# Splitting decoded weights and the gate's sigmoids placed behind the PSUM evictions, and weights decoded 512 columns at a time

## The chip, the cores and the metric

The kernel runs on one core of one Trainium2 chip. The metric is the device time of one execution in microseconds (us). PE is the tensor engine, DVE the vector engine, ACT the scalar engine, POOL is GpSimd, and SP issues the DMAs. Each engine works through its own list of instructions in order. An instruction that waits holds up everything behind it on its engine.

## The reference

Three blocks follow each other for a batch of 4, with 8 heads, 576 positions, head size 64 and 512 channels.

```python
# attention: one full softmax over 4-fold averaged q, k, v, repeated 4 times,
# plus one softmax over the band |i - j| < 4
attn_out = out_up + out_local                      # x: (4, 576, 512)
# gate
gate = sigmoid(causal depthwise conv of x, 5 taps)
x = (gate * (x @ w_val)) @ w_out
# mixing over positions, then over channels
h = relu(x.T @ w_tok1) @ w_tok2                    # 576 -> 256 -> 576
u = x + h.T
out = u + relu(u @ w_ch1) @ w_ch2                  # 512 -> 1536 -> 512
```

The weights of the last two blocks are float64 in memory; all else is float32.

## The kernel before, in words

**Products in three passes.** Each large operand is kept as two tiles: `hi`, the value rounded to the format that PE multiplies fast, and `lo`, the rest. `mm3` adds hi·hi, hi·lo and lo·hi (lines 194, 195 and 196), so each product of a tile is three matmuls.

**Decoding weights.** `decode` fetches a chunk of float64 words into a tile `w64` (named `w` in the trace), lets DVE put together the float32 bits in a tile `wa` by three instructions (L124, L125, L127), lets ACT copy these into `hi` with rounding (L130), and lets POOL subtract to get `lo` (L131). The buffers `w64` and `wa` exist `NWD` times each. A chunk is `WB` columns wide. `w_ch1` is decoded block by block during batch 0 (`ch1_new`, 12 blocks `f`, tile `w_hl`) and written to DRAM (`w_dr`); later batches read it back. Blocks are asked for `AHEAD` = 4 ahead of use. `w_ch2` (tile `ch`) is decoded late in the program.

**Stages.** Attention of batch 0 runs by itself (0 to about 83 us), with idle matmuls on PE between its pieces (`busy`). Then a program of PE's instructions, fixed by hand, runs over the batches: `p1(b)` (value product `p_val`, gate, output product `p_x`, transposes, `r_ps`, `p_h`) and `c1(b)` (the products `g_ps` with `w_ch1`), with the attention of batch `b+1` mixed in at fixed places. The last product with `w_ch2` (`p_o`) fills the time from about 512 us on. PE's order is written out by `mix` and `first_products`. The order on the other engines is made by a scheduler from the order of the code and priorities (`tc.high_priority`).

**Evictions.** ACT takes finished sums out of PSUM: `u_sb` (L494), `x_hl` of the transposes (L504), `r_hl` (L543), `r_sb` (L585), and the attention's `pts_d`, `pts_l` (L295, L343). PE cannot reuse a bank before its eviction. ACT also takes the exponentials of the softmax (`e_d`, `e_l`, L234) and the sigmoids of the gate (L375). Exponential and sigmoid live in different function tables; each change between them is one `ACT_TABLE_LOAD`.

**DVE** besides the decoding does the maxima `mx` of the softmax (L228), the sums `x_f` (L360), the convolution `gate_sb` (L365, L370), the gated product `y` (L481), `lo` parts, and `u_sb` + `p_h` (L558).

Of the kernel before, what the change touches and what calls it, by code (L numbers as in the profile page):

```python
# [34 lines left out]
TAPS = 5  # L35
WB = 256
NW = 16
# [14 lines left out]
FETCH = 10  # L52
NW0, NW1 = 8, 3
NXY = 2
# [5 lines left out]
NPT = 3  # L60
NY = 3
NV = 2
NV4 = 1
ND = 2
NVD = 2
NWD = 3
NX2 = 4
# [7 lines left out]
def kernel(ctx, tc, qk, vw, v4, w_val, conv_w, w_out, w_tok1, w_tok2, w_ch1, w_ch2, out):  # L75
# [25 lines left out]

    idle = T(sb, [128, 512], BF16, "idle", 1, name="idle")
    nc.vector.memset(idle, 0.0)

    def busy(n):
        for _ in range(n):
            p = T(ps, [128, 512], F32, "ao", BANKS["ao"], name="idle_ps")
            nc.tensor.matmul(p, lhsT=idle[:, 0:128], rhs=idle, start=True, stop=True)

# [4 lines left out]

    def decode(src, n, rows, hi, lo, full=None, shape=None):
        x = T(sb, [128, n, 2], I32, "w64", NWD, name="w64")[0:rows]
        a = T(sb, [128, n], I32, "wa", NWD, name="wa")[0:rows]
        if shape is None:
            nc.sync.dma_start(out=x, in_=src.bitcast(I32).rearrange("p (n t) -> p n t", t=2))
        else:  # L120
            nc.sync.dma_start(out=x.rearrange("p (k n) t -> p k n t", k=shape[0]),
                              in_=src.bitcast(I32).rearrange("p k (n t) -> p k n t", t=2))
        low, high = x[:, :, 0], x[:, :, 1]
        nc.vector.tensor_scalar(a, high, 3, 0x3FFFFFF8, ALU.logical_shift_left, ALU.bitwise_and)  # L124
        nc.vector.scalar_tensor_tensor(out=a, in0=high, scalar=-0x40000000, in1=a,  # L125
                                       op0=ALU.bitwise_and, op1=ALU.bitwise_or)
        nc.vector.scalar_tensor_tensor(out=a if full is None else full.bitcast(I32), in0=low, scalar=29, in1=a,  # L127
                                       op0=ALU.logical_shift_right, op1=ALU.bitwise_or)
        if full is None:
            nc.scalar.activation(out=hi, in_=a.bitcast(F32), func=AF.Copy)  # L130
            nc.gpsimd.tensor_tensor(out=lo, in0=a.bitcast(F32), in1=hi.bitcast(F32), op=ALU.subtract)  # L131

    def load_w(key, pieces, tag, bufs, parts=None):

        for j, group in enumerate(pieces):
            n = group[0][1].shape[1]
            hi, lo = parts or [T(sb, [128, len(group), n], F32R, tag, bufs, name=f"{key}{j}_{p}") for p in ("hi", "lo")]
            for i, (rows, src) in enumerate(group):
                for c in range(0, n, WB):
                    e = min(n, c + WB)  # L140
# [33 lines left out]
    def ch2_new():  # L174
# [3 lines left out]
        for tag, bufs in slots:  # L178
            if tag == "w2":
                pairs = [[T(sb, [128, 1, DM], F32R, tag, bufs, name=f"ch2_{f}_{p}")[:, 0] for p in range(2)]]  # L180
            else:
                n = 1 if tag == "wt1" else 2
                t = T(sb, [128, n, 2, DM], F32R, tag, bufs, name=f"ch2_{f}")
                pairs = [[t[:, i, p] for p in range(2)] for i in range(n)]
            for hl in pairs:
                wt["ch2", f] = hl
                for c in range(0, DM, 256):
                    decode(w_ch2[f * 128:f * 128 + 128, c:c + 256], 256, 128, *[t[:, c:c + 256] for t in hl])
                    yield
# [51 lines left out]
    def attention(b):  # L241
# [89 lines left out]
        def loc_turn(hp):  # L331
# [3 lines left out]
            for c0, c1 in LU:  # L335
# [6 lines left out]
                with early():  # L342
                    nc.scalar.activation(out=t, in_=p, func=AF.Copy)  # L343
                ts += [t[:, j] for j in range(n)]

        def loc_out(hp):
# [3 lines left out]
            for j, t in enumerate(ts):  # L350
                for par in range(2):
                    r0 = 64 * par
                    for h in range(2):
                        nc.tensor.matmul(ps_o[par][64 * h:64 * h + 64, j, :],
                                         lhsT=v[r0:r0 + 64, j, 64 * h:64 * h + 64],
# [16 lines left out]

        def sigmoid(s0=0, s1=S):
            for g in g_t:
                nc.scalar.activation(out=g[:, s0:s1], in_=g[:, s0:s1], func=AF.Sigmoid)  # L375

        if b:
# [5 lines left out]
            for i in range(NHP + 1):  # L383
# [20 lines left out]
                if i + 1 < NHP:  # L404
                    hpd[i + 1]["v"] = load_v(b, i + 1)
            sigmoid()
            return

        L = 2
        for hp in range(NHP + L):  # L410
# [11 lines left out]
            if hp >= L:  # L422
# [6 lines left out]
                if hp == NHP + L - 1:  # L429
                    conv(hp - L, 0, HS)  # L430
                    sigmoid(0, HS)
                    conv(hp - L, HS, S)
                else:
                    conv(hp - L)
                yield
        sigmoid(HS, S)
        yield
# [25 lines left out]
    def p1(b):  # L463
# [12 lines left out]
        def val(hs, c, x, y2):  # L476
            p = bank(P1T["p_val"], "p_val")
            cxs(p, wv, x, c)
            with first():
# [4 lines left out]
        def outs(hs, y2):  # L484
            for c0 in (0, 2):
# [83 lines left out]
    def c1(b):  # L569
# [6 lines left out]
        for f in range(NFT):  # L576
            w1 = ws.pop(f)
            r = T(sb, [128, S], F32, "r", 2, name="r_sb")
            for hs in range(2):
# [143 lines left out]
```

## Time and profile before

| | |
|---|---|
| median of 3 runs | 666.13 us (665.65 to 666.78) |
| profiled execution | 664.67 us |
| its span, first to last instruction | 662.8 us |
| PE busy | 622.3 us, 94% |
| DVE, ACT, POOL busy | 339.4, 316.4, 210.0 us |
| mean granted TensorE clock | 0.972 |

The span is what the trace shows; 1.9 us of the execution lie outside it. The profiled execution is 1.5 us under the median of the runs. Busy times of different engines overlap. A clock of 1.00 is 2.4 GHz and 0.50 is 1.2 GHz, so a mean below 1 says for how much of the time PE ran at the lower level.

### The profile page before, as it was taken

Reading aid. Unit: us, or ns where it says so; the run is one execution under the profiler, and the core shown is the slowest. Engines: PE = TensorE matmul, PEld = TensorE weight load, DVE = VectorE, ACT = ScalarE, POOL = GpSimd, SP = SyncE. Lnnn points to the kernel's source line nnn. Section 1 sums busy time; section 2 is a strip of 40 time slices with the busy share of each in tenths; the row PEclk is TensorE's granted clock in tenths of the full one; section 3 lists DMA queues with packets and bytes.
Section 4 is the critical chain, followed back from the end, with each engine's and each line's share of the span. In section 5 each row is a group of like instructions: output and inputs, shape, how many; then the busy total and the mean of one; then the engine's idle time right before and its main releaser. Section 6 shows DMA issues by size and latency. Waiting matters only on the chain.

```text
span 662.8 us, 12825 instructions
## 1 busy us (share of the span) xinstructions
PE 622.3 (94%) x4911; PEld 529.6 (80%) x4911; DVE 339.4 (51%) x630; ACT 316.4 (48%) x1044; POOL 210.0 (32%) x242
## 2 busy tenths in 40 slices
PE   8999778897979999999999999999998999999997
PEld 3444477785878988998998999998897888888887
DVE  3679999775686465442344434117635242324232
ACT  1758457485548586546656843324433222222221
POOL 5564655336536422614231323205513000000000
PEclk8999798797979999999999999999999999999999
DMA  7744226623675244784322586565898345454221
GB/s 254 235 143 117 76 81 205 217 75 122 221 244 178 87 150 131 242 245 124 105 72 72 146 255 203 160 195 187 252 355 272 96 144 174 142 176 127 80 74 38
DMA packets 53900, 107.23 MB, mean 162 GB/s; under 512 B 5776, under 2 KB 21392, under 8 KB 53840
## 3 DMA queue, kind: packets, MB, share of 16 engines
q1 hardware_dynamic: 53840, 106.42, 51.1%
q8 instruction: 38, 0.62, 0.4%
q14 instruction: 22, 0.18, 0.1%
HBM read 76.52 MB, written 29.88 MB: 161 GB/s over the span
## 4 chain that ended last, share of the span: by engine, by line
PE 60%; DVE 6%; DMA 5%; ACT 3%; issue 2%; POOL 1%; SPq 0%; DVEq 0%; ACTq 0%
PE p_o L194 7%; PE p_o L196 7%; PE p_o L195 7%; PE g_ps L194 5%; PE g_ps L195 5%; PE g_ps L196 5%; DMA w<-in_w_ch_dram 4%; PE sc_l L325 2%; PE p_x L194 2%; DVE wa L124 2%; PE p_x L195 2%; PE p_x L196 2%; PE p_val L194 2%; PE p_val L196 2%; PE p_val L195 2%
## 5 line engine op out<-in xcount | busy, mean ns | idle before, releaser
L194 PE MATMUL g_ps<-u_hl,w_hl 128*128 128x288 f32 x384 | 117.8, 307 | 0.0
L195 PE MATMUL g_ps<-u_hl,w_hl 128*128 128x288 f32 x384 | 115.0, 299 | 2.1 <-POOL u_hl L444 1.9
L196 PE MATMUL g_ps<-u_hl,w_hl 128*128 128x288 f32 x384 | 113.9, 297 | 0.0
L194 PE MATMUL p_o<-g_hl,ch 128*128 128x512 f32 (+1 forms) x240 | 88.8, 370 | 2.2 <-ACT r_sb L585 2.1
L196 PE MATMUL p_o<-g_hl,ch 128*128 128x512 f32 (+1 forms) x240 | 88.5, 369 | 0.0
L195 PE MATMUL p_o<-g_hl,ch 128*128 128x512 f32 (+1 forms) x240 | 88.5, 369 | 0.0
L443 ACT ACTIVATE g_hl<-r_back 128x512 fp32r<-128x512 f32 (+1 forms) x60 | 35.3, 589 | 109.1 <-PE p_o L196 106.3
L444 DVE TENSOR_TENSOR g_hl<-r_back,g_hl 128x512 fp32r<-128x512 f32 (+1 forms) x60 | 39.4, 658 | 92.8 <-ACT g_hl L443 89.6
L195 PEld LDWEIGHTS g_ps<-u_hl,w_hl 128*128 128x128 f32 x384 | 73.3, 191 | 3.5 <-POOL u_hl L444 3.5
L194 PEld LDWEIGHTS g_ps<-u_hl,w_hl 128*128 128x128 f32 x384 | 73.1, 190 | 3.1 <-issue 1.7
L196 PEld LDWEIGHTS g_ps<-u_hl,w_hl 128*128 128x128 f32 x384 | 73.2, 191 | 0.0
L370 DVE SCALAR_TENSOR_TENSOR gate_sb<-x_f,cw,gate_sb 128x575 f32<-128x575 f32 (+5 forms) x68 | 62.8, 930 | 1.5 <-ACT gate_sb L367 0.5
L585 ACT ACTIVATE r_sb<-g_ps 128x288 f32<-128x288 f32 x96 | 38.2, 406 | 47.0 <-PE g_ps L196 41.2
L124 DVE TENSOR_SCALAR wa<-w 128x256 int32<-128x256 int32 (+2 forms) x76 | 37.1, 499 | 34.8 <-DMA w<-in_w_ch_dram 21.1
L194 PEld LDWEIGHTS p_o<-g_hl,ch 128*128 128x128 f32 x240 | 45.2, 188 | 10.8 <-ACT r_sb L585 3.2
L196 PEld LDWEIGHTS p_o<-g_hl,ch 128*128 128x128 f32 x240 | 45.2, 188 | 7.7
L195 PEld LDWEIGHTS p_o<-g_hl,ch 128*128 128x128 f32 x240 | 45.3, 189 | 7.6
L234 ACT ACTIVATE e_l<-sc_l,mx 128x64 f32<-128x64 f32 x160 | 48.1, 331 | 0.4
L194 PE MATMUL p_x<-y_hl,out_hi 128*128 128x288 f32 x128 | 40.9, 320 | 4.2 <-ACT u_sb L494 3.7
L125 DVE SCALAR_TENSOR_TENSOR wa<-w,wa 128x256 int32<-128x256 int32 (+2 forms) x76 | 44.2, 591 | 1.1
L444 POOL TENSOR_TENSOR x_hl<-x_f,x_hl 128x288 fp32r<-128x288 f32 x32 | 27.7, 877 | 45.5 <-ACT x_hl L443 44.8
L194 PE MATMUL p_val<-x_hl,val_hi 128*128 128x288 f32 x128 | 39.5, 309 | 1.4 <-DVE y L481 0.7
(108 smaller groups left out, 1354.0 us busy)
## 6 DMA issues: line engine op xcount, KB each, us to landing
w_hl<-w_dr SPq DMA_DIRECT2D x36, 512.0 KB, 4.6
r_dr<-r_sb SPq DMA_DIRECT2D x48, 288.0 KB, 4.6
w<-in_w_ch_dram SPq DMA_DIRECT2D x48, 256.0 KB, 3.4
r_back<-r_dr SPq DMA_DIRECT2D x48, 256.0 KB, 3.0
qk_sb<-in_qk_dram SPq DMA_DIRECT2D x16, 589.0 KB, 4.0
w_dr<-w_hl SPq DMA_DIRECT2D x12, 512.0 KB, 3.0
v_sb<-in_vw_dram SPq DMA_DIRECT2D x16, 320.0 KB, 4.0
v_sb<-in_v_dram SPq DMA_DIRECT2D x16, 288.0 KB
```

What stands on the lines that cost most here:

```text
L124: nc.vector.tensor_scalar(a, high, 3, 0x3FFFFFF8, ALU.logical_shift_left, ALU.bitwise_and)
L125: nc.vector.scalar_tensor_tensor(out=a, in0=high, scalar=-0x40000000, in1=a, op0=ALU.bitwise_and, op1=ALU.bitwise_or)
L194: nc.tensor.matmul(out_ap, lhsT=lh, rhs=rh, start=first, stop=False)
L195: nc.tensor.matmul(out_ap, lhsT=lh, rhs=rl, start=False, stop=False)
L196: nc.tensor.matmul(out_ap, lhsT=ll, rhs=rh, start=False, stop=last)
L234: nc.scalar.activation(out=e[:, o, :], in_=p[:, c, :], func=AF.Exp, scale=scale, bias=mx[:, o:o + 1], accum_out=sm[:, o:o + 1])
L325: nc.tensor.matmul(p[r0:r0 + 64, c, :], lhsT=qk[r0:r0 + 64, 0, 3 + o:3 + o + WIN], rhs=qk[r0:r0 + 64, 1, o:o + WIN], start=False, stop=(c ...
L370: nc.vector.scalar_tensor_tensor(out=g[:, t0:s1], in0=x[:, t0 - sh:s1 - sh], scalar=cw[:, hp, k:k + 1], in1=g[:, t0:s1], op0=ALU.mult, op1 ...
L443: nc.scalar.activation(out=hi_ap, in_=src_ap, func=AF.Copy)
L444: lo_eng.tensor_tensor(out=lo_ap, in0=src_ap, in1=hi_ap.bitcast(F32), op=ALU.subtract)
L585: nc.scalar.activation(out=r[:, hv(hs)], in_=p[:, 0:HS], func=AF.Relu)
```

## The change

Six things change; PE's own work in the fixed program stays the same instructions in the same order.

1. A chunk is 512 columns wide (`WB`), `w_tok2` in chunks of 288. The buffers `w64` and `wa` are now two each (`NWD`).
2. Where a block's DVE part is done, its ACT copy and POOL subtraction (`split`) are no longer issued at once. They wait in `pending` and are issued when the next block is decoded, and the ACT copy is placed on ACT behind the last eviction that the program has written so far (`paced`). The write of `w_ch1`'s block to DRAM waits in the same list.
3. The sigmoids of batches 1 to 3 are issued together: three at the end of the batch's attention and the last one in `p1`, all behind the last eviction. Those of batch 0 come behind the last `pts_l`.
4. The first value product of batch 0 starts on PE behind the last `o_l` product of its attention.
5. The idle matmuls are 224 columns instead of 512, and twice as many.
6. `y32` has two buffers instead of three.

```diff
-WB = 256
+WB = 512
-NW0, NW1 = 8, 3
+NW0, NW1 = 16, 6
-NY = 3
+NY = 2
-NWD = 3
+NWD = 2
...
+    paced, pending = [None], []
+    def behind_pace():
+        return tc.issue_after(paced[0].ins) if paced[0] else nullcontext()
+    def flush():
+        while pending:
+            with behind_pace():
+                pending.pop(0)()
...
-        if full is None:
+        def split():
             nc.scalar.activation(out=hi, in_=a.bitcast(F32), func=AF.Copy)
             nc.gpsimd.tensor_tensor(out=lo, in0=a.bitcast(F32), in1=hi.bitcast(F32), op=ALU.subtract)
+        if full is None:
+            if paced[0]:
+                if not keep:
+                    flush()
+                pending.append(split)
+            else:
+                split()
...
-        for c in range(0, KC, 2):
-            decode(src[:, c:c + 2], 256, 128, *[t[:, i, c * 128:c * 128 + 256] for i in range(2)], shape=(2, 128))
-        nc.sync.dma_start(out=w1_dr[:, f], in_=t.bitcast(F32))
+        decode(src, DM, 128, t[:, 0], t[:, 1], shape=(KC, 128))
+        pending.append(lambda: nc.sync.dma_start(out=w1_dr[:, f], in_=t.bitcast(F32)))
...
-        def sigmoid(s0=0, s1=S):
-            for g in g_t:
-                nc.scalar.activation(out=g[:, s0:s1], in_=g[:, s0:s1], func=AF.Sigmoid)
+        def sigmoid(s0=0, s1=S, hps=range(NHP), behind=None):
+            for hp in hps:
+                with tc.issue_after((behind or paced[0]).ins):
+                    g = g_t[hp][:, s0:s1]
+                    nc.scalar.activation(out=g, in_=g, func=AF.Sigmoid)
...
-            sigmoid()
+            sigmoid(hps=range(NHP - 1))
+            last_gate[b] = lambda: sigmoid(hps=(NHP - 1,))
...
+            if c == 2 and b:
+                last_gate.pop(b)()
             val(0, c, x, y2)
```

The line numbers of the changed kernel differ: the decode's lines are 135, 136 and 138 on DVE and 142 on ACT, `u_sb` is 520, `r_sb` 615, the sigmoid 399, `pts_l` 364, the exponential 255, `r_hl` 572, the sum with `p_h` 586, and the `x_f` sum 381.

How the orders move is shown at three places. The first is ACT while PE waits for `pts_l` near the end of `c1(0)`, where the last head pair of batch 1's attention runs. Before:

```order
L130 ACTIVATE w_hl<-wa 128x256 [waits DVE_49]
L375 ACT_TABLE_LOAD
L375 ACTIVATE gate_sb<-gate_sb 128x576 [waits DVE_49]
L585 ACTIVATE r_sb<-g_ps 128x288 [waits DMAHW2_49,PE_49,Activation_49]
L343 ACTIVATE pts_l<-pt_l 128x384 [waits PE_49]
L343 ACTIVATE pts_l<-pt_l 128x256 [waits PE_49,Activation_49]
```

In the changed kernel, from the eviction ahead of the same `pts_l`:

```order
L615 ACTIVATE r_sb<-g_ps 128x288 [waits DMAHW6_49,PE_49,Activation_49]
L364 ACTIVATE pts_l<-pt_l 128x384 [waits PE_49]
L364 ACTIVATE pts_l<-pt_l 128x256 [waits PE_49,Activation_49]
L615 ACTIVATE r_sb<-g_ps 128x288 [waits PE_49]
L142 ACTIVATE w_hl<-wa 128x512 [waits DMAHW1_49,DVE_49,Pool_49]
L468 ACTIVATE x_hl<-x_f_1207 128x288 [waits DVE_49]
L615 ACTIVATE r_sb<-g_ps 128x288 [waits DMAHW2_49,PE_49]
L615 ACTIVATE r_sb<-g_ps 128x288 [waits PE_49]
L142 ACTIVATE w_hl<-wa 128x512 [waits DMAHW5_49,Pool_49]
L399 ACT_TABLE_LOAD
L399 ACTIVATE gate_sb<-gate_sb 128x576 x3
L399 ACTIVATE gate_sb<-gate_sb 128x576 [waits DVE_49]
```

The copy of decoded weights, the table load and the sigmoid have moved from ahead of `pts_l` to behind it, and the four sigmoids now stand at the start of batch 1's `p1`, in front of its first `y_hl`.

The second place is ACT at the evictions of `p_x` of batch 0 (from 90 us on). Before:

```order
L130 ACTIVATE tok_hl<-wa 128x256 [waits DVE_49]
L494 ACTIVATE u_sb<-p_x_1064 128x288 [waits PE_49]
L130 ACTIVATE tok_hl<-wa 128x256 [waits DVE_49]
L494 ACTIVATE u_sb<-p_x_1065 128x288 [waits PE_49]
L130 ACTIVATE tok_hl<-wa 128x64 [waits DVE_49]
L130 ACTIVATE tok_hl<-wa 128x256 [waits DVE_49]
L494 ACTIVATE u_sb<-p_x_1100 128x288 [waits PE_49]
```

In the changed kernel:

```order
L520 ACTIVATE u_sb<-p_x_1142 128x288 [waits PE_49]
L520 ACTIVATE u_sb<-p_x_1143 128x288 [waits PE_49]
L520 ACTIVATE u_sb<-p_x_1178 128x288 [waits PE_49]
L251 ACTIVATE mx<-mx 72x4 [waits DVE_49]
L520 ACTIVATE u_sb<-p_x_1179 128x288 [waits PE_49]
L255 ACT_TABLE_LOAD
L255 ACTIVATE e_d,sm<-sc_d,mx 72x144 [waits Activation_49]
```

The copies that wait for DVE are gone from between the evictions; the table load ahead of `e_d` stays.

The third place is DVE at `p_h` of batch 0 (141 to 152 us). Before, no decoding stands there:

```order
L228 TENSOR_REDUCE mx<-sc_l 128x6 [waits PE_49]
L228 TENSOR_REDUCE mx<-sc_l 128x4 [waits PE_49]
L505 TENSOR_TENSOR x_hl<-x_ps,x_hl 64x512 [waits Activation_49]
L238 RECIPROCAL sm<-sm 72x4 [waits Activation_49]
L544 SCALAR_TENSOR_TENSOR r_hl<-r_ps,r_hl 128x512 [waits Activation_49] x2
L266 TENSOR_REDUCE qk_d<-qk_sb 128x288 [waits DMAHW5_49]
L558 TENSOR_TENSOR u_sb<-p_h,u_sb 128x288 [waits PE_49] x3
```

In the changed kernel:

```order
L572 SCALAR_TENSOR_TENSOR r_hl<-r_ps,r_hl 128x512 [waits Activation_49]
L287 TENSOR_REDUCE qk_d<-qk_sb 128x288 [waits DMAHW5_49]
L572 SCALAR_TENSOR_TENSOR r_hl<-r_ps,r_hl 128x512 [waits Activation_49]
L586 TENSOR_TENSOR u_sb<-p_h,u_sb 128x288 [waits PE_49]
L135 TENSOR_SCALAR wa<-w_1712 128x512 [waits DMAHW7_49,Pool_49]
L136 SCALAR_TENSOR_TENSOR wa<-w_1712,wa 128x512 [waits DVE_49]
L586 TENSOR_TENSOR u_sb<-p_h,u_sb 128x288 [waits PE_49] x2
L138 SCALAR_TENSOR_TENSOR wa<-w_1712,wa 128x512 [waits DVE_49]
```

The decoding of a block of `w_ch1` has moved in among the sums that free `p_h`'s banks. Its first instruction waits for a DMA and for POOL's subtraction of an earlier block, which has to release the buffer `wa`. And `qk_d` stands between the two `r_hl`.

## Rows read from the trace of the kernel before

**Rows 1.** The page's head, its engine rows and clock slices.

```profile
span 662.8 us, 12825 instructions
...
PE 622.3 (94%) x4911; PEld 529.6 (80%) x4911; DVE 339.4 (51%) x630; ACT 316.4 (48%) x1044; POOL 210.0 (32%) x242
...
PEclk8999798797979999999999999999999999999999
```

**Rows 2.** Who waited for whom on PE: us in total, times, longest us.

```profile
PE sc_l L319 <- ACT e_d L234: 6.2, 4, 2.6
PE p_x L194 <- ACT u_sb L494: 3.7, 4, 2.3
PE o_l L354 <- ACT pts_l L343: 3.6, 1, 3.6
...
PE p_o L194 <- ACT r_sb L585: 2.1, 2, 1.2
...
PE p_h L194 <- DVE u_sb L558: 1.8, 3, 1.1
```

**Rows 3.** Windows: engine busy us (instructions), granted clock, DMA share, GB/s.

```profile
100.00:120.00 20.00, 17.20 (x176) 14.69 (x175) 19.22 (x43) 12.60 (x62) 10.28 (x12) 0.91 0.69 220
...
120.00:140.00 20.00, 18.27 (x165) 15.54 (x166) 14.78 (x24) 12.40 (x44) 4.11 (x5) 0.83 0.44 129
...
160.00:180.00 20.00, 17.83 (x186) 15.77 (x186) 10.96 (x21) 11.53 (x51) 10.27 (x12) 0.86 0.55 189
...
180.00:200.00 20.00, 16.38 (x141) 15.68 (x140) 17.82 (x36) 8.76 (x21) 8.63 (x10) 0.83 0.72 238
...
520.00:540.00 20.00, 20.00 (x89) 16.51 (x88) 4.86 (x7) 4.45 (x8) 0.00 (x0) 1.00 0.34 97
```

**Rows 4.** Timeline of ACT around 184 us: start, us, instruction, idle before.

```profile
184.04 0.42 ACT L130 ACTIVATE w_hl<-wa 128x256 fp32r<-128x256 f32 x1 [3.12 <-DVE wa L127]
184.47 1.28 ACT L375 ACT_TABLE_LOAD   x1
185.77 0.68 ACT L375 ACTIVATE gate_sb<-gate_sb 128x576 f32<-128x576 f32 x1
```

**Rows 5.** Timeline of PE: the same product at 146 and at 187 us.

```profile
146.27 0.81 PE L354 MATMUL o_l<-pts_l,v_sb 64*64 64x58 f32 x40
...
187.18 1.60 PE L354 MATMUL o_l<-pts_l,v_sb 64*64 64x58 f32 x40 [3.62 <-ACT pts_l L343]
```

**Rows 6.** Timeline of ACT from 90 to 98 us.

```profile
90.61 0.42 ACT L130 ACTIVATE tok_hl<-wa 128x256 fp32r<-128x256 f32 x1 [1.97 <-DVE wa L127]
...
97.42 1.28 ACT L234 ACT_TABLE_LOAD   x1
```

**Rows 7.** Timeline of DVE at the end of batch 0's attention.

```profile
59.27 0.83 DVE L360 TENSOR_TENSOR x_f<-o_l,x_f 128x290 f32<-128x290 f32 x2 [0.31 <-PE o_l L354]
...
77.01 0.81 DVE L360 TENSOR_TENSOR x_f<-o_l,x_f 128x290 f32<-128x290 f32 x2
...
82.43 0.44 DVE L481 TENSOR_TENSOR y<-p_val,gate_sb 128x288 f32<-128x288 f32 x1
```

**Rows 8.** DVE's groups by line, 59.2 to 82.5 us: busy us, mean ns, idle before.

```profile
L124 DVE TENSOR_SCALAR wa<-w 128x256 int32<-128x256 int32 x5 | 3.4, 704 | 1.0 <-POOL out_lo L131 1.0
L127 DVE SCALAR_TENSOR_TENSOR wa<-w,wa 128x256 int32<-128x256 int32 x5 | 3.1, 638 | 0.0
L125 DVE SCALAR_TENSOR_TENSOR wa<-w,wa 128x256 int32<-128x256 int32 x5 | 3.0, 634 | 0.0
```

**Rows 9.** Groups by line and shape, whole span, and one DMA row.

```profile
L504 ACT ACTIVATE x_hl<-x_ps 128x512 fp32r<-128x512 f32 x16 | 9.6, 603 | 12.7 <-PE x_ps L501 12.7
...
L131 POOL TENSOR_TENSOR w_hl<-wa,w_hl 128x256 fp32r<-128x256 f32 x24 | 19.9, 845 | 31.1 <-ACT w_hl L130 31.1
...
w_hl<-w_dr SPq DMA_DIRECT2D x36, 512.0 KB, 4.6
```

**Rows 10.** Timeline of DVE at the first `p_h` of batch 0.

```profile
142.73 1.34 DVE L266 TENSOR_REDUCE qk_d<-qk_sb 128x288 f32<-128x1152 f32 x1
```

More of the change, by code (lines that the diff above doesn't have):

```diff
@@ L99 @@
     cw = T(sb, [128, KC, TAPS], F32, "cw", 1)
-    idle = T(sb, [128, 512], BF16, "idle", 1, name="idle")
+    idle = T(sb, [128, 224], BF16, "idle", 1, name="idle")
     nc.vector.memset(idle, 0.0)
@@ L107, in busy, with decode @@
             p = T(ps, [128, 512], F32, "ao", BANKS["ao"], name="idle_ps")
-            nc.tensor.matmul(p, lhsT=idle[:, 0:128], rhs=idle, start=True, stop=True)
+            nc.tensor.matmul(p[:, 0:224], lhsT=idle[:, 0:128], rhs=idle, start=True, stop=True)
     wt = {k: [] for k in ("val", "out", "tok1", "tok2")}
-    def decode(src, n, rows, hi, lo, full=None, shape=None):
-        x = T(sb, [128, n, 2], I32, "w64", NWD, name="w64")[0:rows]
-        a = T(sb, [128, n], I32, "wa", NWD, name="wa")[0:rows]
+    paced, pending = [None], []
[5 more added lines that the diff above has]
+                pending.pop(0)()
+    def decode(src, n, rows, hi, lo, full=None, shape=None, keep=0):
+        x = T(sb, [128, WB, 2], I32, "w64", NWD, name="w64")[0:rows, 0:n]
+        a = T(sb, [128, WB], I32, "wa", NWD, name="wa")[0:rows, 0:n]
         if shape is None:
@@ L138, in load_w @@
             for i, (rows, src) in enumerate(group):
-                for c in range(0, n, WB):
-                    e = min(n, c + WB)
+                w = n if n <= WB else n // 2
+                for c in range(0, n, w):
+                    e = c + w
                     decode(src[:, c:e], e - c, rows, hi[0:rows, i, c:e], lo[0:rows, i, c:e])
@@ L186, in ch2_new @@
                 wt["ch2", f] = hl
-                for c in range(0, DM, 256):
-                    decode(w_ch2[f * 128:f * 128 + 128, c:c + 256], 256, 128, *[t[:, c:c + 256] for t in hl])
-                    yield
+                decode(w_ch2[f * 128:f * 128 + 128], DM, 128, *hl)
+                yield
                 f += 1
+        flush()
     def mm3(out_ap, lhs, rhs, first, last):
@@ L199 @@
     xf, gate = {}, {}
+    last_gate, last_copy, last_pe = {}, [None], [None]
     LU = [(0, 6), (6, 10)]
@@ L342, in loc_turn @@
                 with early():
-                    nc.scalar.activation(out=t, in_=p, func=AF.Copy)
+                    last_copy[0] = nc.scalar.activation(out=t, in_=p, func=AF.Copy)
                 ts += [t[:, j] for j in range(n)]
@@ L353, in loc_out @@
                     for h in range(2):
-                        nc.tensor.matmul(ps_o[par][64 * h:64 * h + 64, j, :],
+                        last_pe[0] = nc.tensor.matmul(ps_o[par][64 * h:64 * h + 64, j, :],
                                          lhsT=v[r0:r0 + 64, j, 64 * h:64 * h + 64],
@@ L430, in attention @@
                     conv(hp - L, 0, HS)
-                    sigmoid(0, HS)
+                    sigmoid(0, HS, behind=last_copy[0])
                     conv(hp - L, HS, S)
@@ L435, in attention @@
                 yield
-        sigmoid(HS, S)
+        sigmoid(HS, S, behind=last_copy[0])
         yield
@@ L477, in val @@
             p = bank(P1T["p_val"], "p_val")
-            cxs(p, wv, x, c)
+            with tc.issue_after(last_pe[0].ins) if b + hs + c == 0 else nullcontext():
+                cxs(p, wv, x, c)
             with first():
@@ L493, in outs @@
                     for c in range(2):
-                        nc.scalar.activation(out=u[:, c0 + c, hv(hs)], in_=ps_x[c][:, 0:HS], func=AF.Copy)
+                        paced[0] = nc.scalar.activation(out=u[:, c0 + c, hv(hs)], in_=ps_x[c][:, 0:HS], func=AF.Copy)
                 yield 6 * MM
@@ L503, in transposed @@
                 t = x2[s] = T(sb, [128, 2, DM], F32R, "x2r", NX2, name="x2_hl")
-                nc.scalar.activation(out=t[0:n, 0], in_=p[0:n], func=AF.Copy)
+                paced[0] = nc.scalar.activation(out=t[0:n, 0], in_=p[0:n], func=AF.Copy)
                 nc.vector.tensor_tensor(out=t[0:n, 1], in0=p[0:n], in1=t[0:n, 0].bitcast(F32), op=ALU.subtract)
@@ L542, in p1 @@
                 t = T(sb, [128, 2, DM], F32R, "x2r", NX2, name="r_hl")
-                nc.scalar.activation(out=t[:, 0], in_=rp[m], func=AF.Relu)
+                paced[0] = nc.scalar.activation(out=t[:, 0], in_=rp[m], func=AF.Relu)
                 nc.vector.scalar_tensor_tensor(out=t[:, 1], in0=rp[m], scalar=0.0, in1=t[:, 0].bitcast(F32),
@@ L577, in c1 @@
             w1 = ws.pop(f)
+            if b == 0 and f == NFT - AHEAD:
+                flush()
             r = T(sb, [128, S], F32, "r", 2, name="r_sb")
@@ L584, in c1 @@
                 with tc.high_priority(offset=PRI):
-                    nc.scalar.activation(out=r[:, hv(hs)], in_=p[:, 0:HS], func=AF.Relu)
+                    paced[0] = nc.scalar.activation(out=r[:, hv(hs)], in_=p[:, 0:HS], func=AF.Relu)
                 if hs:
@@ L675 @@
     last = c2()
-    side += [(ch2_new(), 24, *W2_AT), (last, 1, C2_AT, C2_AT + 1)]
+    side += [(ch2_new(), 12, *W2_AT), (last, 1, C2_AT, C2_AT + 1)]
     with tc.manual_schedule(engines={mybir.EngineType.PE}):
```

## The prediction

> **What bounds the kernel now.** I read the page first, then PE's waits, then the windows, then the timelines at the places the waits point to. The page shows PE busy for 622.3 of 662.8 us, so PE sets the time and 40.5 us is all that its idle time holds [rows 1]. From 520 us on PE is busy for all of each window (20.00 of 20) at full clock [rows 3]; nothing is to be had there. What can move lies ahead of 240 us, where PE's share is lower and the clock slices drop below 9 [rows 1].
>
> The waits name the evictions on ACT as the largest group: `sc_l` behind `e_d` 6.2 us, `p_x` behind `u_sb` 3.7, `o_l` behind `pts_l` 3.6, `p_o` behind `r_sb` 2.1 [rows 2]. ACT is not short of time (316.4 us busy [rows 1]). It is held up: at 184.04 it has stood idle for 3.12 us in front of a weight copy that waits for DVE, then loads a table for 1.28 us and takes a sigmoid, and `pts_l`, for which PE waits, comes only then [rows 4]. The same happens in front of `u_sb` at 90.61 (ACT idle 1.97 us behind DVE) [rows 6].
>
> The second loss is the clock. In the windows 100:120, 120:140, 160:180 and 180:200 it is 0.91, 0.83, 0.86 and 0.83 [rows 3]. The `o_l` product of 40 matmuls takes 0.81 us at 146.27 but 1.60 us at 187.18, right behind PE's wait of 3.62 us [rows 5]. So a long wait is paid twice. At full speed throughout, the four windows would need at most (0.09 + 0.17 + 0.14 + 0.17) x 20 = 11.4 us less, if PE were busy in all of the slow time.
>
> **The change part by part.** The sum is made against the profiled execution of 664.67 us.
>
> *Evictions on ACT.* In the order of the changed kernel the weight copy, table load and sigmoid stand behind `pts_l`, and the weight copies are gone from between the `u_sb`. Term by term: of `sc_l`'s 6.2 us I keep one table load, which still stands ahead of `e_d` at 97.42 (1.28 us [rows 6]), and take 4.9. Of `p_x`'s 3.7 us I keep 1.0 for the longest wait, where `u_sb` stands behind exponentials too (fewer now, but some), and take 2.7. Of `o_l`'s 3.6 us, everything ahead of `pts_l` in [rows 4] goes, and I take 3.3. Of `p_o`'s 2.1 us I take 1.5, because the `ch` copies now stand behind pairs of `r_sb`, not between them. Together 12.4 us. The bounds are 7 (the shorter waits find another cause) and 13.
>
> A table load costs 1.28 us by the row: 184.47 + 1.28 is 185.75 and the sigmoid starts at 185.77 [rows 4]. The Trainium skill ("ScalarE: Activation LUTs", section "What ACT_TABLE_LOAD costs") adds a drain of about 1.38 us to each load, 2.66 us in all. No such gap stands behind the load in this trace, so the measurement decides. By the page the load that stays ahead of `e_d` and the three at the starts of batches would cost 4 x 1.38 = 5.5 us more, an estimate from that page.
>
> *Clock.* If the long waits at 158 to 161 and 183 to 187 us go, so should the slow stretches behind them: 0.14 + 0.17 of 20 us is 6.2, of which I take 85% since PE also idles there, 5.3 us. Of the two earlier windows, (0.09 + 0.17) x 20 = 5.2 us, I take half, 2.6, because shorter waits stay there. Together 7.9; bounds 0 and 11.4.
>
> *End of batch 0's attention.* DVE works from the `x_f` at 59.27 to the first `y` at 82.43 with hardly a break, 23.2 us [rows 7]. In it stand 15 decode instructions, 3.4 + 3.1 + 3.0 = 9.5 us, and 1.0 us of waiting for POOL [rows 8]. In the changed order four are left there, some 4 x 0.66 = 2.6 us by the same rows, so up to 9.5 + 1.0 - 2.6 = 7.9 us can go. Against it, the first half's sigmoids now stand in one batch with a table load ahead of the last `x_hl` and the last convolution: 1.28 us and three half sigmoids of less than 0.68 each [rows 4], some 3 us, and PE may idle there. I take 5; bounds 0 and 8. The idle matmuls hide nothing that the end of the stage depends on, so I cost them, like `NY`, at nothing: they fill time in which PE waits, and without that cover PE would only be idle instead.
>
> *What it adds.* (a) At the start of batches 1 to 3 ACT does a weight copy (0.60 us for 512 columns, by the `x_hl` copy [rows 9], in batch 1 only), a table load and a sigmoid, 1.28 + 0.68 [rows 4], before the first `y` can be formed. PE has two value products to do meanwhile, 24 matmuls. From 89 matmuls of 512 columns in 20.00 us [rows 3] one is 0.225 us, 288 columns by proportion 0.126, so 24 take 3.0 us. The `y` itself takes 0.44 [rows 7], and the last eviction ahead of the copy about as long, so the sum on ACT's side is 3.4 us against 3.0: about 0.3 us a batch, 1.0 in all (0 to 2.5).
>
> (b) At `p_h` of batch 0 the convenience of an empty DVE goes. `qk_d`, 1.34 us [rows 10], now stands between the two `r_hl`, so the second comes that much later: 1.3 us. Behind the first `u_sb` of `p_h` stands a decode whose first instruction waits for a DMA and for POOL. Two decode instructions stand ahead of the next `u_sb`. For 512 columns I have only the 256-column rows, 0.63 to 0.70 us each where POOL is at work [rows 8]; twice that is the upper bound, once the lower. I take 0.9. The two products that PE can run ahead cover part: 1.7 us. Together 3.0 (0 to 6, if the DMA is late too; `p_h` already waits 1.8 us for these sums [rows 2]).
>
> (c) The other places where a decode stands ahead of an `x_f`, a `mx` or a sum with `p_h`: 1.5 us (0 to 4), from one or two further decode instructions of 0.9.
>
> The POOL subtraction is the same number of columns in fewer pieces, and DVE saves the fixed part of the smaller instructions. DVE, ACT and POOL are not the bound, so their totals are worth nothing beyond the terms above.
>
> The sum: 12.4 + 7.9 + 5 - 1.0 - 3.0 - 1.5 = 19.8 us off 664.67, so 644.9 profiled. The profiled execution lies 1.5 us under the median of the runs, so I predict 646.3.
>
> **The rivals.**
>
> *Waits pass to DVE.* With two `wa`, DVE's in-order list waits at each decode for POOL's subtraction, which waits for the ACT copy, which waits behind an eviction, which waits for PE. Sums with `p_h`, `x_f` and `mx` stand behind it. If this doubles (b) and (c), to 9 us, and the waits it makes are long enough to leave the clock low (3 us back instead of 7.9), the sum is 12.4 + 3 + 4 - 1 - 9 = 9.4, giving 656.7. For it: the order puts a decode into `p_h`, where none stood. Against: blocks are asked for four ahead.
>
> *Slower: the decode of `w_ch1` falls behind.* A block's `wa` is held for three DVE instructions (2.7 us), the time until the next block releases the split (up to a block), an ACT copy of 0.60 and a subtraction of 0.845 to 1.7 us [rows 9]. At a pace of 3.5 us a block (24 matmuls, 3.0, and the attention between) this is 8.2 us for two buffers, 4.1 us a block. The `w64` side is a 512 KB transfer, 4.6 us [rows 9], and 2.7 of DVE for two buffers: 3.65. Twelve blocks at 4.1 fall 11 x 0.6 = 6.6 us behind, which a lead of two blocks, 7 us, just covers. If a block takes 6 us, 11 x 2.5 - 7 = 20.5 us of waits appear, no clock comes back, and the sum is 12.4 + 5 - 2.5 - 20.5 = -5.6, giving 671.7. It decides from about 5.6 us a block on. DVE's instructions or the transfer would have to take half as long again as these rows say.
>
> *No gain at the start.* If the last head pair's chain over ACT and PE, not DVE, sets the end of the attention, 5 us go: 651.3. For it: the table load and sigmoids ahead of the last `x_hl`.
>
> *Everything.* All of the clock (11.4), start 8, waits 13, costs 3: 29.4 us, 636.7.
>
> *It changes nothing.* The copies are behind evictions in the order already printed, so this needs gains and costs to cancel, or the waits on ACT to be replaced one for one.
>
> *Longer table loads*, the case of the page: if a load held ACT for twice what [rows 4] shows, four times 1.3 us would go, 651.5. [Rows 4] speaks against it.
>
> **How the numbers follow.** Chances: forecast 0.40, everything 0.15, no start gain 0.12, longer loads 0.03, waits pass to DVE 0.16, no change 0.05, slower 0.09. The low end, 635, is just below the case of everything; the high end, 661, takes in the case of DVE's waits with its clock and costs at their bounds and leaves out the last two and a tail of each. The forecast's own range is 640 to 652. A measurement here can tell about 0.2%, 1.3 us. Faster by more than that: 0.86; within it 0.05; slower 0.09.
>
> **What would show it.** In the changed profile `o_l` behind `pts_l` should be gone from PE's waits and `sc_l` behind `e_d` be down to about one table load's worth. The windows 160:200 should be at full clock. The first `y` should come near 77 us. New rows should be `p_h` behind `u_sb` or `r_hl` on DVE, some 3 us, and `p_val` behind `y` at the starts of batches, some 0.3 each. I am wrong if a wait on DVE's decode or on the transfer appears that is over 2 us long, or if low clock stays in those windows without one.

## The result, and the profile after

The changed kernel takes 674.25 us (median of 6, 670.82 to 676.10) against 665.89 us before (median of 6): ratio 1.0119, 95% interval 1.0092 to 1.0147. It is slower by 1.2%, where 646.3 was forecast. The profiled execution has a span of 674.0 us, 11.2 more than before. The medians are 8.4 us apart, so some 3 us of what is read below off these two executions is spread between executions.

The page of the changed kernel, head, engines and clock slices, to be read against [rows 1]:

```profile
span 674.0 us, 12692 instructions
...
PE 630.7 (94%) x4982; PEld 541.3 (80%) x4982; DVE 320.2 (48%) x528; ACT 297.5 (44%) x998; POOL 204.4 (30%) x208
...
PEclk9988797888998999999999999999899999999999
```

DVE and ACT each work 19 us less. On ACT 15.4 us of that are table loads: 8 of 1.28 us, where there were 20. The clock is low over more of the front. PE's waits in the changed kernel (us, times, longest):

```profile
PE p_val L214 <- DVE y L507: 5.8, 1, 5.8
PE o_l L375 <- ACT pts_l L364: 4.3, 3, 3.7
...
PE p_x L214 <- ACT u_sb L520: 3.6, 2, 2.2
...
PE pt_d L313 <- DVE x_f L381: 2.3, 1, 2.3
...
PE p_h L214 <- DVE u_sb L586: 1.7, 2, 1.0
PE sc_l L340 <- ACT e_d L255: 1.5, 3, 1.0
PE p_h L214 <- DVE r_hl L572: 1.3, 1, 1.3
PE p_o L214 <- ACT r_sb L615: 1.1, 1, 1.1
```

Against [rows 2], `sc_l` has gone from 6.2 to 1.5 and `p_o` from 2.1 to 1.1. `p_x` has nearly the same total, but not at the same places: before, 3.5 us of it lay between 90 and 125 us, where now there is none, and now 2.2 us lie between 125 and 160 us and 1.4 us in batch 2's part. On top stands a wait that is new at this length: `p_val` for `y` on DVE (0.7 us before). Windows of the changed kernel (columns as in [rows 3]):

```profile
60.00:80.00 20.00, 15.04 (x152) 9.71 (x153) 14.60 (x23) 9.73 (x36) 9.88 (x10) 0.66 0.32 93
...
160.00:180.00 20.00, 18.19 (x177) 15.77 (x174) 11.04 (x17) 11.66 (x49) 10.65 (x10) 0.83 0.56 203
180.00:200.00 20.00, 14.69 (x146) 13.45 (x145) 19.93 (x27) 9.54 (x21) 7.50 (x7) 1.00 0.75 265
200.00:220.00 20.00, 16.92 (x136) 15.12 (x137) 8.88 (x17) 12.90 (x50) 12.09 (x14) 0.83 0.42 132
```

In 180:200 DVE is busy for 19.93 of 20 us, where it was 17.82 [rows 3]. The timeline of DVE in the changed kernel, the first `y` and the stretch up to batch 1's first `y`:

```profile
88.96 0.44 DVE L507 TENSOR_TENSOR y<-p_val,gate_sb 128x288 f32<-128x288 f32 x1
...
176.55 0.22 DVE L259 RECIPROCAL sm<-sm 128x10 f32<-128x10 f32 x1 [5.78 <-ACT sm L258]
...
192.41 0.81 DVE L381 TENSOR_TENSOR x_f<-o_l,x_f 128x290 f32<-128x290 f32 x2
...
193.69 0.42 DVE L135 TENSOR_SCALAR wa<-w 128x512 int32<-128x512 int32 x1
...
195.32 1.79 DVE L136 SCALAR_TENSOR_TENSOR wa<-w,wa 128x512 int32<-128x512 int32 x1
...
197.76 0.68 DVE L138 SCALAR_TENSOR_TENSOR wa<-w,wa 128x512 int32<-128x512 int32 x1
...
199.10 0.41 DVE L135 TENSOR_SCALAR wa<-w 128x512 int32<-128x512 int32 x1
...
201.16 1.21 DVE L136 SCALAR_TENSOR_TENSOR wa<-w,wa 128x512 int32<-128x512 int32 x1
202.30 0.81 DVE L507 TENSOR_TENSOR y<-p_val,gate_sb 128x288 f32<-128x288 f32 x2
```

DVE works from 177.48 to the two `y` at 202.30 without a break. Just before, it stood idle for 5.78 us until ACT had its sums `sm` ready. And of the kernel before, batch 1's first `y`:

```profile
195.62 0.46 DVE L481 TENSOR_TENSOR y<-p_val,gate_sb 128x288 f32<-128x288 f32 x1
```

Two events read off these rows divide the 11.2 us. The first `y` moved from 82.43 [rows 7] to 88.96: 6.5 us later. From there to batch 1's first `y` is 113.2 us before (195.62 - 82.43) and 113.3 now: nothing gained and nothing lost. After it 4.5 us more are lost: 1.6 up to batch 2's first `y` (105.1 us before, 106.7 now), behind the wait for batch 1's `y` and in the slow clock of 200:220, and 2.9 in pieces later.

PE itself did get further in the middle. These are batch 1's first value product before and, in the changed kernel, the first and the third:

```profile
193.83 0.30 PE L194 MATMUL p_val<-x_hl,val_hi 128*128 128x288 f32 x1
```

```profile
193.33 0.29 PE L214 MATMUL p_val<-x_hl,val_hi 128*128 128x288 f32 x1
...
202.80 0.61 PE L214 MATMUL p_val<-x_hl,val_hi 128*128 128x288 f32 x1 [5.84 <-DVE y L507]
```

Counted from batch 0's first `y`, PE comes to batch 1's first value product after 111.4 us before and after 104.4 now. So 7.0 us were won up to there, and the wait of 5.84 us for `y` and the slow clock behind it take them back. Two questions are open: what delays the start, and why does `y` come no sooner although ACT's waits went?

### The profile page after: what moved, and what is told of

Its sections match the earlier page's. It is cut to its first block, busy times and chain, and to the rows that moved or that the text cites. A ratio compares the mean times of both kernels' runs of the same rounds, so it can differ in the third digit from the quotient of the medians.

```text
span 674.0 us, 12692 instructions
## 1 busy us (share of the span) xinstructions
PE 630.7 (94%) x4982; PEld 541.3 (80%) x4982; DVE 320.2 (48%) x528; ACT 297.5 (44%) x998; POOL 204.4 (30%) x208
## 4 chain that ended last, share of the span: by engine, by line
PE 74%; DVE 10%; ACT 6%; POOL 4%; issue 3%; DMA 3%; SPq 0%; POOLq 0%; ACTq 0%; DVEq 0%
PE p_o L214 7%; PE p_o L216 7%; PE p_o L215 7%; PE g_ps L214 6%; PE g_ps L215 5%; PE g_ps L216 5%; PE idle_ps L108 3%; PE sc_l L346 3%; PE qk_d L284 3%; PE p_x L214 2%; PE p_val L214 2%; DVE gate_sb L391 2%; PE p_val L215 2%; PE p_val L216 2%; DMA w<-in_w_ch_dram 2%
## 5 line engine op out<-in xcount | busy, mean ns | idle before, releaser
L216 PE MATMUL g_ps<-u_hl,w_hl 128*128 128x288 f32 x384 | 114.3, 298 | 0.0
L391 DVE SCALAR_TENSOR_TENSOR gate_sb<-x_f,cw,gate_sb 128x575 f32<-128x575 f32 (+5 forms) x68 | 67.7, 1003 | 3.2 <-ACT gate_sb L388 2.2
L135 DVE TENSOR_SCALAR wa<-w 128x512 int32<-128x512 int32 (+4 forms) x42 | 27.3, 654 | 47.5 <-DMA w<-in_w_ch_dram 21.5
L469 POOL TENSOR_TENSOR u_hl<-u_sb,u_hl 128x288 fp32r<-128x288 f32 x32 | 27.4, 866 | 54.6 <-ACT u_hl L468 54.6
```

Of the source, the lines that this page charges most:

```text
L216: nc.tensor.matmul(out_ap, lhsT=ll, rhs=rh, start=False, stop=last)
L391: nc.vector.scalar_tensor_tensor(out=g[:, t0:s1], in0=x[:, t0 - sh:s1 - sh], scalar=cw[:, hp, k:k + 1], in1=g[:, t0:s1], op0=ALU.mult, op1 ...
L469: lo_eng.tensor_tensor(out=lo_ap, in0=src_ap, in1=hi_ap.bitcast(F32), op=ALU.subtract)
```

## The experiments

**One part alone, four kernels.** The first changes only the idle matmuls of the kernel before:

```diff
-NW0, NW1 = 8, 3
+NW0, NW1 = 16, 6
...
-    idle = T(sb, [128, 512], BF16, "idle", 1, name="idle")
+    idle = T(sb, [128, 224], BF16, "idle", 1, name="idle")
...
-            nc.tensor.matmul(p, lhsT=idle[:, 0:128], rhs=idle, start=True, stop=True)
+            nc.tensor.matmul(p[:, 0:224], lhsT=idle[:, 0:128], rhs=idle, start=True, stop=True)
```

> The kernel before with only the idle matmuls changed (16 and 6 of 224 columns in place of 8 and 3 of 512). Theory A, the idle matmuls make the longer start: the first value product comes later than in the kernel before and TensorE's clock falls to half between 40 and 75 us, as in the changed kernel; 670 to 673 us. Rival B, the wide decode chunks make it: no difference beyond 1.5 us, 665 to 667 us.

Measured: 678.99 us, ratio 1.0204 (1.0160 to 1.0247). Theory A holds, and more strongly than it said: the first `y` is at 95.69, 13.3 us later than before. The timeline of PE shows where it begins; first the kernel before, then this one:

```profile
38.59 2.55 PE L108 MATMUL idle_ps<-idle 128*128 128x512 bf16 x6
41.20 3.29 PE L263 MATMUL qk_d<-qk_sb,ident 128*128 128x288 f32 x6
```

```profile
38.75 0.55 PE L339 MATMUL pt_l<-ident,e_l 128*128 128x128 f32 x3
41.54 0.48 PE L319 MATMUL sc_l<-mask,ident 128*128 128x384 bf16 x1 [2.24 <-ACT e_l L234]
...
47.87 2.79 PE L263 MATMUL qk_d<-qk_sb,ident 128*128 128x288 f32 x5
```

The scheduler orders PE in batch 0's attention. With other idle matmuls it put `sc_l`, which must wait for a bank, ahead of `qk_d`, which need not. PE idles 2.24 us and `qk_d` comes 6.7 us later. In 60:80 this kernel's clock is 0.50, where it was 0.83:

```profile
60.00:80.00 20.00, 18.74 (x143) 10.77 (x143) 7.84 (x17) 13.23 (x46) 8.33 (x10) 0.50 0.21 57
```

The second has only the sigmoids placed (`issue_after` the last eviction, as in the diff):

> The kernel before with only the sigmoids placed behind the evictions. Theory A, the wait of 5.8 us for the first gated product of batch 1 comes from DVE's decode: the table loads ahead of PE's waits at 158 and 184 us are gone, no such wait appears, 658 to 662 us. Rival B, it comes from the sigmoids' new place: the wait appears here, 666 to 672 us.

Measured: 663.99 us, ratio 0.997 (0.994 to 1.000). Between the two ranges. Its waits show both at once: the waits of 2.6 and 3.6 us behind table loads are gone, and this one is new:

```profile
PE p_val L195 <- DVE y L487: 4.5, 1, 4.5
```

Its first `y`s are 112.7 us apart (83.14 and 195.83).

The third has only the wide chunks (`WB` 512, `NWD` 2, `NY` 2):

> The kernel before with only the chunks of 512 columns, two buffers for them and two for y32 (ACT's copy at once, idle matmuls of 512 columns read from a smaller tile). Theory A, the wide pieces in DVE's order cost: first gated product of batch 1 late by 3 to 8 us, 668 to 674 us. Rival B, the deferral costs and not the width: 664 to 667 us. If the wide chunks also make the longer start, the first value product is 4 to 6 us later.

Measured: 668.63 us, ratio 1.0032 (1.0014 to 1.0051). That is the low end of A's range, and batch 1's first `y` is late by 5.0 us (200.60), as A said. But the delay is there from the start: the first `y` is at 87.27, 4.8 us later than before, and the two are 113.3 us apart. So the wide chunks make the start longer too.

The fourth has only `pending`, `flush` and `behind_pace`:

> The kernel before with only the deferred ACT copies and subtractions (chunks of 256 columns, three buffers). Theory A, the deferral itself is good and the width spoils it: ACT's copies are gone from ahead of u_sb and pts_l, 658 to 663 us. Rival B, the deferral pushes the decode into later stages and DVE's order: waits at p_h of batch 0 and at the start of batch 1, 667 to 672 us.

Measured: 665.09 us, ratio 0.9986 (0.9966 to 1.0006). Neither: no gain, no loss, and first `y`s 113.2 us apart (81.75 and 194.99). The two parts that were to bring 20 us bring 0 to 2 each.

**Idle matmuls put back, and their size.** The changed kernel with idle matmuls of 512 columns, 128 columns read four times:

```diff
-NW0, NW1 = 16, 6
+NW0, NW1 = 8, 3
...
-    idle = T(sb, [128, 224], BF16, "idle", 1, name="idle")
+    idle = T(sb, [128, 128], BF16, "idle", 1, name="idle")
...
-            nc.tensor.matmul(p[:, 0:224], lhsT=idle[:, 0:128], rhs=idle, start=True, stop=True)
+            nc.tensor.matmul(p.rearrange("p (a w) -> p a w", a=4), lhsT=idle, rhs=idle.unsqueeze(1).to_broadcast([128, 4, 128]), start=True, stop=True)
```

> The changed kernel with the idle matmuls of the kernel before (8 and 3 of 512 columns, read from a smaller tile, since the large one doesn't fit beside the wide chunks). Theory A, the idle matmuls cost the changed kernel what they cost alone, some 13 us: first value product near 78 to 82 us, 659 to 664 us. Rival B, in the changed kernel the wide chunks hold the start back too: 668 to 673 us.

Measured: 670.32 us, ratio 1.0075 (1.0047 to 1.0103), 3.9 us under the changed kernel by the medians and 2.9 by the ratios. The first `y` is at 84.81, so 4.2 us of the start come back. That is rival B: in the changed kernel the idle matmuls cost 3 to 4 us, not 13.

Then the kernel before with idle matmuls of 448 columns, and of 224, both 8 and 3 times:

> The kernel before with idle matmuls of 448 columns, as many as before (8 and 3): per step the same columns as 6 of 224. Theory A, the narrow matmuls cost because twice as many stand in TensorE's list and take longer (0.165 us each against 0.22 for 512), or because the list is put in another order: 663 to 668 us. Rival B, it is the smaller number of columns: 674 to 680 us.

> The kernel before with idle matmuls of 224 columns, as many as before (8 and 3), so half the columns and about half the idle matmuls' time of the changed kernel. Theory A, the time that they take in TensorE's list is what costs: 660 to 666 us. Rival B, the clock falls where fewer columns are worked on: half clock over more than 14 us between 40 and 90 us, 670 to 682 us.

Measured: 669.95 (ratio 1.0070, 1.0043 to 1.0097) and 669.44 us (1.0061, 1.0042 to 1.0081). Neither lies in a range of A, and the second just misses B's. Both cuts of the columns cost some 4 us. The first has as many columns per step as the narrow matmuls of the first experiment and costs a third of them, so the number of columns alone doesn't set the price. The start is 2.4 and 0.4 us later than before (first `y`s at 84.83 and 82.84). More is lost up to batch 1's first `y` (201.13 and 200.95), 3.1 and 4.9 us: that distance has grown to 116.3 and 118.1 us, and DVE works 89.4 and 93.7 us in it, against 87.6 before.

Last, order and length apart. With the instructions of PE and DVE in batch 0's attention in written order, 512 and 224 columns give the same order on all engines:

```diff
-    mix((1 for _ in a[0]), [(w, 6, V0, V1), ((busy(NW1) for _ in range(21)), 21, 0, 21)])
+    E = mybir.EngineType
+    with tc.manual_schedule(engines={E.PE, E.DVE}):
+        mix((1 for _ in a[0]), [(w, 6, V0, V1), ((busy(NW1) for _ in range(21)), 21, 0, 21)])
```

> The kernel before with the instructions of PE and DVE in batch 0's attention in the order in which the code writes them, so that the lengths of the idle matmuls can't move anything; idle matmuls of 512 columns, 8 and 3. It is the base for the next run; its own time may be 662 to 685 us.

> As the run before it, with the idle matmuls of the changed kernel (224 columns, 16 and 6). All engines have the same order in both. Theory A, the idle matmuls cost through the order that the scheduler makes with them: within 3 us of the run with 512 columns. Rival B, they cost by themselves, by their own time on PE or by the clock: 6 to 13 us more.

Measured: 688.54 and 694.70 us, 6.2 more for 224 columns. Rival B. So the idle matmuls cost in equal order too. Whether they take as much of the 13 us in the kernel before is not shown, since these two kernels are themselves 22 us and more slower than it. In the traces, which are 7.4 us apart, the difference is spread: 3.6 us up to the first `y` (98.71 and 102.33), 1.2 up to batch 1's first, 2.5 later. The wait ahead of the second `sc_d`, first with 512, then with 224 columns, is one piece.

```profile
24.33 1.24 PE L279 MATMUL sc_d<-qk_d 64*72 64x144 f32 x8 [3.79 <-ACT qk_d L264]
```

```profile
25.36 1.00 PE L279 MATMUL sc_d<-qk_d 64*72 64x144 f32 x6 [5.92 <-ACT qk_d L264]
```

**Where the gains on ACT go.** Deferral, sigmoids and the first value product together, chunks and idle matmuls as before:

> The kernel before with the deferred copies, the placed sigmoids and the first value product behind the last o_l product, but chunks of 256 columns with three buffers and the idle matmuls of before. Theory A, DVE's list sets the end of batch 0's channel product, so that what ACT gains is given back in waits for DVE: the first value product of batch 1 ends within 3 us of the kernel before, 661 to 665 us. Rival B, the two gains add up as predicted: 645 to 655 us.

Measured: 666.15 us, ratio 1.0015 (0.9995 to 1.0035). Rival B is out. It is theory A, 1.2 us above its range: the first `y`s stand at 83.01 and 196.95, 113.9 us apart. To test DVE, one of the three decode instructions is left out, with the lowest three bits of each weight:

```diff
-        nc.vector.scalar_tensor_tensor(out=a if full is None else full.bitcast(I32), in0=low, scalar=29, in1=a,
-                                       op0=ALU.logical_shift_right, op1=ALU.bitwise_or)
+        if full is not None:
+            nc.vector.scalar_tensor_tensor(out=full.bitcast(I32), in0=low, scalar=29, in1=a,
+                                           op0=ALU.logical_shift_right, op1=ALU.bitwise_or)
```

> The kernel before with two of the three DVE instructions of each weight decode (the lowest three bits of each float32 weight are left out). It is the base for the next run. Theory A, DVE's list sets the end of batch 0's part: a few us less, 660 to 664 us, though ACT's placing still holds some of it. Rival B, ACT's evictions bound it: 664 to 667 us.

> The kernel with deferred copies and placed sigmoids (chunks of 256) with two of the three DVE instructions of each decode (the lowest three bits of each float32 weight are left out). Theory A, what ACT gains is given back in DVE's list: with less in that list the gain shows, 6 us or more under the run with all three instructions, 650 to 660 us, and more under it than the kernel before gains by the same cut. Rival B, PE's chain or POOL takes over: 663 to 667 us.

> The changed kernel with idle matmuls of 512 columns (8 and 3) and two of the three DVE instructions of each decode (the lowest three bits of each float32 weight are left out). Theory A, what the wide chunks cost beyond the deferral is also DVE's list: 10 to 16 us under the same kernel with three instructions, 655 to 660 us. Rival B, it is the longer hold of two buffers (DMA, subtraction): under 6 us less, 664 us or more.

Measured:

| | three instructions | two instructions |
|---|---|---|
| kernel before | 665.96 us, 1 | 661.54 us, 0.9930 (0.9901 to 0.9959) |
| deferral and sigmoids | 666.15 us, 1.0015 | 654.59 us, 0.9832 (0.9800 to 0.9865) |
| changed kernel, idle of 512 | 670.32 us, 1.0075 | 656.21 us, 0.9873 (0.9825 to 0.9921) |

Theory A each time. The same cut is worth 0.7% in the kernel before, 1.8% with the deferral and 2.0% with the wide chunks. ACT and POOL have another order in these kernels too, so the numbers hold the shorter decoding together with the order made for it. The first `y`s of the second and the third kernel:

```profile
79.16 0.45 DVE L508 TENSOR_TENSOR y<-p_val,gate_sb 128x288 f32<-128x288 f32 x1
...
188.69 0.81 DVE L508 TENSOR_TENSOR y<-p_val,gate_sb 128x288 f32<-128x288 f32 x2
```

```profile
80.64 0.44 DVE L508 TENSOR_TENSOR y<-p_val,gate_sb 128x288 f32<-128x288 f32 x1
...
188.54 0.45 DVE L508 TENSOR_TENSOR y<-p_val,gate_sb 128x288 f32<-128x288 f32 x1
```

The distance falls from 113.9 to 109.5 us and from 114.3 to 107.9, and the start comes 3.9 and 4.2 us earlier. These are the windows between the two `y`s with deferral and sigmoids, with three instructions and with two (columns as in [rows 3]):

```profile
83.01:196.95 113.94, 97.85 (x890) 86.13 (x888) 88.06 (x174) 63.78 (x238) 52.51 (x57) 0.90 0.50 161
```

```profile
79.16:188.69 109.53, 94.62 (x887) 84.31 (x885) 77.71 (x144) 63.52 (x238) 54.86 (x59) 0.91 0.52 167
```

DVE has 10.4 us less work there, and the stretch is 4.4 us shorter.

**Relief for DVE with nothing left out**, on the kernel with deferral and sigmoids: the first tap of the convolution on ACT for batch 1, for batches 1 to 3, and for batch 1 with the sums for `qk_d` on POOL.

```diff
-            if b:
+            if b > 1:
                 nc.vector.tensor_scalar(g[:, s0:s1], x[:, s0:s1], cw[:, hp, TAPS - 1:TAPS], None, ALU.mult)
```

The second kernel has `if False:` there. The third has `b > 1`, and for batch 1 three additions on `gpsimd` in place of the sum of four on DVE.

> The kernel with deferred copies and placed sigmoids (chunks of 256, idle matmuls of 512), with the first tap of batch 1's convolution on ACT in place of DVE; nothing is left out. Theory A, every us taken from DVE's list ahead of batch 1 counts: 4 instructions of 0.5 to 1 us less, 2 to 4 us under the run without it, 661 to 664 us. Rival B, ACT is now as full there as DVE: 665 us or more.

> As the run before it, with the first tap of the convolutions of batches 1 to 3 on ACT. Theory A, only batch 1's part is bound by DVE: the same as the run before it within 1.5 us. Rival B, the later batches gain too: 2 us or more under it.

> The kernel with batch 1's first tap on ACT, and also batch 1's sums of four for q and k on POOL (three additions each in place of one DVE reduction of 1.34 us); nothing is left out. Theory A, DVE's list counts: 3 to 6 us under the run with the tap alone, 656 to 661 us. Rival B, POOL's longer list delays the lo parts and the releases of the decode's buffers, and slows DVE beside it: 665 us or more.

Measured: 663.23 us (ratio 0.9978, 0.9957 to 0.9998), 664.36 (0.9996, 0.9976 to 1.0016) and 666.25 (1.0022, 1.0003 to 1.0040). The first is 2.9 us under the run without it, in A's range. But its first `y`s stand at 83.35 and 197.33, again 114.0 us apart, and the gain comes behind them, so not where A put it. The second is like it; A again. The third is in B's range, 3.0 us above the first. Its first `y`s stand at 86.53 and 198.52: the stretch between them is 2.0 us shorter, and the start 3.2 us later, where POOL already makes the sums of two head pairs (from 47.1 us on). In sum the work moved to POOL costs more than it frees. The first is the only full computation here whose interval lies below 1, and only just.

## Why the prediction was wrong

*The idle matmuls.* The step that failed first is "The idle matmuls hide nothing that the end of the stage depends on, so I cost them, like `NY`, at nothing". Alone they cost 2.0%, in the changed kernel 3 to 4 us. Two things were missed. The scheduler plans batch 0's attention with their lengths, so other lengths gave another order on PE and ACT; that is so even with 448 columns, where nothing but the length differs. And in equal order they still cost 6.2 us. Why, stays open: in that pair their time on PE is much the same (23.9 us for the 68 of 71 that the trace has, and 25.9), and so is the clock of the first 100 us, 0.81 with 512 columns and 0.83 with 224.

*End of batch 0's attention.* Forecast 5 us earlier, it came 6.5 later. With the idle matmuls put back it is 2.4 later (84.81 against 82.43), and with the wide chunks alone 4.8, so the term was wrong in sign without them too. DVE was relieved, as worked out, and then it no longer set the end. In the changed kernel it waits there for PE and ACT:

```profile
75.57 0.83 DVE L381 TENSOR_TENSOR x_f<-o_l,x_f 128x290 f32<-128x290 f32 x2 [1.10 <-PE o_l L375]
...
82.41 0.83 DVE L381 TENSOR_TENSOR x_f<-o_l,x_f 128x290 f32<-128x290 f32 x2 [0.62 <-PE o_l L375]
...
84.60 4.44 DVE L391 SCALAR_TENSOR_TENSOR gate_sb<-x_f,cw,gate_sb 128x287 f32<-128x287 f32 x6 [1.37 <-ACT gate_sb L388]
```

That is the mechanism of the rival "No gain at the start", a chain over ACT and PE; the place that it named, the table load and the sigmoids, holds the last 1.37 us. The chain itself had become longer ahead of these rows, at a place that I had left out: PE waits 3.7 us for `pts_l` up to 62.84. With the idle matmuls put back that wait is 4.6 us, and with the wide chunks alone PE waits 4.8 us just ahead of the same product.

*Evictions on ACT, 12.4 us, and clock, 7.9 us.* The waits did go where they were read: `sc_l` is down by 4.7 (4.9 forecast), `p_o` by 1.0 (1.5), and the wait of 3.6 us for `pts_l` at 183 is gone; the 3.7 us now listed for it stand in the start. `p_x`'s 3.5 us at 90 to 125 us went too, but 3.6 us came up at two other places. The failure is in adding these to the end of the stage. DVE's list, in which decode, convolution and `y` stand in order, was nearly as late as ACT's; the row at 184.04 says so, since ACT itself stands there for 3.12 us behind DVE's decode [rows 4]. With ACT out of the way the same end is set by DVE: 113.2 us before, 112.7 with the sigmoids alone, 113.9 with deferral and sigmoids, 113.3 in the changed kernel. The wait of 5.8 us for `y` takes the place of the 3.6 and 2.6 us that had gone; where only the sigmoids moved, the same two went and 4.5 us for `y` came. Then the clock falls behind it, and over the whole execution it is 0.961 where it was 0.972, so nothing of that term was earned.

*What it adds.* (b), at `p_h` of batch 0: forecast 3.0 us, shown 2.5 where 0.3 was before (1.3 and 0.5 behind `r_hl`, 0.7 behind `u_sb`); right in place and near in size. The 1.8 us of [rows 2], which I took to be at this place, lie after 440 us. (a), the sigmoids at the start of a batch: the place was right and the reason wrong. ACT had finished the three sigmoids at 197.96; `y` stood on DVE behind the convolution of the last head pair and five decode instructions, 0.42 + 1.79 + 0.68 + 0.41 + 1.21 = 4.5 us. (c) was sized at 1.5 us and holds this 5.8 us and the 2.3 us at `pt_d` (1.4 before).

*The rivals.* "Waits pass to DVE", given 0.16 and 656.7 us, names the right engine, as the runs with two instructions show, but not the reason: between the two first `y`s of the changed kernel DVE waits only 1.7 us for POOL to release a buffer (2.5 us for POOL before), and its list is late by its own instructions. Its price was too low, because I let it double a cost that I had sized from the new places only, not from the end of DVE's list. Its sum also takes 4 us for the start where the forecast takes 5, and the sum of the rival below it leaves out (b), both without a reason. "The decode of `w_ch1` falls behind" through its two buffers is not what the trace shows: in the changed kernel PE never waits for `w_hl`, and beside those 1.7 us DVE waits 0.9 us for the transfer. The 14 us that two instructions bring with the same two buffers don't decide it, since a shorter decode also holds a buffer for less long. "Longer table loads" is out: in the changed kernel the load at 194.84 takes 1.28 us and the sigmoid starts at 196.13.

*What stays open.* DVE is not busy for all of the 113 us: it works 84.4 of them in the changed kernel, and 7.0 us it waits for ACT's `sm`. Taking 10.4 us of work from it brought 4.4, and the first tap on ACT, some 3 us of DVE, left the distance at 114.0 us and gained elsewhere. So it is shown that less decoding on DVE, with the order made for it, shortens the stage, and not that the sum of DVE's work alone sets it; order, waits and the traffic with POOL have a part that was not separated.

## What to carry to other kernels

Before the waits for one engine are added up as a gain, look at the end of the stage and ask how late every other in-order engine is there. If a second one ends within a few us, the gain is at most that difference. Measure the stage between two events on both kernels: a distance that stays the same while waits come and go says that the bound is elsewhere.

Filler work is not free where a scheduler plans with its length. Change it in a run of its own.

## What had not been expected of the hardware

With all engines in the same order, idle matmuls of 512 columns (8 and 3) and of 224 (16 and 6), an eighth fewer columns in all, differ by 6.2 us over the whole kernel (688.54 and 694.70).

And a 512-column decode instruction on DVE takes 0.68 us at 197.76 but 1.21 and 1.79 at 201.16 and 195.32 for the same kind of work. POOL at that time:

```profile
194.90 1.67 POOL L143 TENSOR_TENSOR w_hl<-wa,w_hl 128x512 fp32r<-128x512 f32 x1
199.26 1.37 POOL L289 TENSOR_TENSOR v_sb<-v_sb 72x512 f32<-72x512 f32 x1 [2.69 <-DMA v_sb<-in_v_dram]
200.71 1.12 POOL L290 TENSOR_TENSOR vd<-v_sb 72x256 f32<-72x256 f32 x1
```

The long ones stand beside a POOL instruction and the short one in POOL's pause. It is so in the whole trace of the changed kernel: of the 64 such instructions (L136 and L138) the 36 without POOL beside them took 0.68 to 0.69 us each, and all of the 17 that took 0.94 us or more had POOL beside them. No run tests it by itself. It bears on the wait for `y`, since two of the five decode instructions ahead of it are long ones.
